# Blocks 2 and 3 of layer one by the seven-product scheme, with attention in another order and W2 jobs converted in another way

## The chip, the cores and the metric

One core of one Trainium2 chip. The metric is the time of one execution in device microseconds; a profile gives in addition the span from the first instruction to the last, the granted TensorE clock and the time of every instruction. TensorE multiplies, VectorE and ScalarE do elementwise work, GpSimd is nearly unused here, and every DMA of the stages below is issued from the SP queue.

## The reference

Chunked attention over 4 x 8 heads of 768 tokens (each chunk of 32 tokens sees 8 memory keys, 16 to the left, itself and 8 to the right), then two feed-forward layers over the 3072 tokens:

```python
scores = scale * np.matmul(q_c, k_full.transpose(0, 1, 3, 2))
a = np.exp(scores - np.max(scores, axis=-1, keepdims=True))
out[:, :, c_start:c_end] = np.matmul(a / (np.sum(a, axis=-1, keepdims=True) + 1e-09), v_full)
...
h = x @ w_in                                          # 3072 x 512 by 512 x 2048
g = np.maximum(h, 0.0) + np.log1p(np.exp(-np.abs(h))) # layer one, softplus
x = g @ w_out                                         # 3072 x 2048 by 2048 x 512
...
g = h - np.tanh(h)                                    # layer two, other weights
return g @ w_out
```

## The kernel before

**Numbers.** Weights, x and g are kept as two parts, a high part in the 32-bit format fp32r (`h`, `gh`) and a low part, the rest (`l`, `gl`). A product of two such operands is three matmuls, high by high, high by low, low by high (`mm3`, L368). Tokens lie in the free dimension, 512 to a block, so every big matmul is 128 x 128 by 128 x 512. `split_g` (L401) and `y_steps` (L677) make the parts of g: a cast on ScalarE gives `gh` (L405, L686), a subtraction on VectorE gives `gl` (L409, and L627 through `minus`). There are three buffers each of `gh` and `gl`.

**Layer one, plain.** For each of the 16 slices f of the hidden dimension, `ff_h` (L377) makes h (4 x 3 = 12 matmuls), ScalarE the softplus, `split_g` the parts, and `ff_y1` (L412) adds the slice's product with W1's output half into four PSUM tiles `ps_y` (12 matmuls). y runs LAG = 2 slices behind h. Blocks 0 to 3 run like this, block 0 inside a written opening.

**Seven products.** Where two blocks are taken together, y is a 2 x 2 block product by Strassen's scheme: seven products q, each over eight slices p instead of sixteen, on sums of the g quarters (`y_steps`, subtractions at L627) and on sums of weight quarters that jobs have stored in DRAM. `y_phase` takes 7 x 8 steps (q, p) of 6 matmuls. Before step s + 3's `gh`/`gl` are made, step s must have let its buffers go: `y_steps` is kept AHEAD = 3 steps ahead. After a product, `after_y` (L700) copies it (`kept`, ScalarE, L618) or adds it to the kept one (VectorE, L711) and stores it. The weight quarters come through a ring of 1 MB halves (`Ring`, L583), each loaded when the half before it in the same buffer is done (DMA of L601). Before, blocks 4 and 5 of layer one and all of layer two run by seven products; h of layer two does too, h of layer one does not. For blocks 4 and 5 all of h is made first (`steps`), into six rotating PSUM tiles, then y.

**Ticks.** The work that isn't the two layers' main stream is laid out by `tick` (L765), called once after every 12 big matmuls; the tables of numbers give the tick of everything:
- attention units 8 to 23 (128 tokens each): scores `s_mm` (L270) and the v product of the unit before (L343) in a unit's first tick, max and subtraction on VectorE (L295, L299), exp on ScalarE (L309) in the next, sum and scaling (L312 to L315) in the third, transposes `t_mm` (L320) and their copy `pT` (L332) in the fifth, x's parts (L358, L360) when the v product is there. A unit takes six ticks; softplus and exp need different tables on ScalarE (ACT_TABLE_LOAD). Units 20, 21 and 22 stand early in the order, and their x goes through DRAM.
- W1 jobs (`job_w1`, L488), which make the sums of W1's quarters; W2 jobs (`job_w`, L441), which load 1 MB of 64-bit floats of layer two's weights, rebuild 32-bit ones from their two words, split and store them, once as they are and once as sums (`split_to`, L428: cast L430, subtraction L434); x jobs (`job_x`, L500), which make the seven sums of layer two's x.

DVE, ACT, PE and SP run in the order in which the code issues. The jobs' results go through a pool of four buffers `o`; a buffer is free again when its store has landed. The W2 job before:

```python
nc.scalar.mul(c.bitcast(F32), hi.bitcast(F32), EXP_BIAS)                     # L450, ScalarE
nc.vector.tensor_scalar(out=c, in0=c, scalar1=3, ...)                        # L452
for of, k, op in ((hi, 0x80000000, and), (lo, 29, logical_shift_right)):
    nc.vector.scalar_tensor_tensor(out=c, in0=of, scalar=k, in1=c, ...)      # L454, twice
```

## Time and profile before

| | |
|---|---|
| median of 3 runs | 1059.66 us (1058.99 to 1059.68) |
| the profiled execution | 1059.62 us |
| its span | 1057.8 us |
| granted TensorE clock, mean | 0.998 |
| TensorE / VectorE / ScalarE busy | 1045.9 / 727.9 / 566.0 us |
| DMA | 303.19 MB, mean 287 GB/s |

The span is what the profile covers; the time of the execution is 1.8 us longer. Busy time of an engine is the union of its instructions. In lists of groups the columns are busy time, mean duration of one, and the idle time of the engine just before them with what ended it; matmuls overlap, so the mean of one matmul (389 ns) is longer than the distance of two.

### The profile page before, as it was taken

The numbers are of one execution on the slowest core, as the hardware profiler recorded it, in microseconds if no ns is written. First come the engines' busy times: TensorE is split into PE (matmuls) and PEld (weight loads), VectorE is DVE, ScalarE is ACT, GpSimd is POOL, SyncE is SP. The second block draws the span as 40 slices with busy tenths as digits, with TensorE's granted clock in tenths as the row PEclk, the third lists the DMA queues.
The fourth block names the chain that finished last, engine by engine and source line by source line (L and its number), as shares of the span: only waits on it lengthen the run. The fifth ranks groups of instructions, "written<-read, shape, count | busy, mean of one in ns | idle before, by whom it ended". The sixth has DMA issues, their size and how long they took to land.

```text
span 1057.8 us, 18468 instructions
## 1 busy us (share of the span) xinstructions
PE 1045.9 (99%) x7380; PEld 856.0 (81%) x7380; DVE 727.9 (69%) x1130; ACT 566.0 (54%) x901; POOL 4.4 (0%) x10
## 2 busy tenths in 40 slices
PE   7999999999999999999999999999999999999998
PEld 4788788888888888888888888888888888888886
DVE  5999355855755657487677688777487877446876
ACT  5996554655555455344555565545455554344553
POOL 1000000000000000000000000000000000000000
PEclk9999999999999999999999999999999999999999
DMA  9999955857776986999988999978899888746661
GB/s 309 409 368 347 350 190 180 285 195 227 265 250 234 308 313 199 356 337 342 327 339 295 351 369 348 342 286 324 285 356 346 287 324 290 246 164 211 244 206 60
DMA packets 101749, 303.19 MB, mean 287 GB/s; under 512 B 8096, under 2 KB 55200, under 8 KB 84000
## 3 DMA queue, kind: packets, MB, share of 16 engines
q1 hardware_dynamic: 101280, 300.97, 79.6%
q10 hardware_dynamic: 384, 1.05, 0.4%
q8 instruction: 58, 0.95, 0.4%
q14 instruction: 27, 0.22, 0.1%
HBM read 211.29 MB, written 90.70 MB: 285 GB/s over the span
## 4 chain that ended last, share of the span: by engine, by line
PE 95%; DMA 2%; ACT 1%; DVE 1%; issue 0%; ACTq 0%; DVEq 0%
PE ps_y L370 46%; PE ps_h L370 31%; PE ps_b L370 13%; PE ps_a L343 2%; PE ps_a L270 1%; DMA w<-in_qk 1%; PE ps_a L320 1%; DMA w<-in_w1i 1%; DMA y1d<-o 0%; PE ps_h L382 0%; PE ps_h L859 0%; ACT sm L304 0%; ACT x L304 0%; ACT x L358 0%; DVE st L295 0%; DVE c L495 0%
## 5 line engine op out<-in xcount | busy, mean ns | idle before, releaser
L370 PE MATMUL ps_h<-x,w 128*128 128x512 f32 x900 | 215.4, 390 | 0.0
L686 ACT CAST gh<-w 128x512 fp32r<-128x512 f32 x224 | 139.3, 623 | 140.0 <-DVE gl L627 120.0
L627 DVE TENSOR_TENSOR gl<-w,gh 128x512 fp32r<-128x512 f32 x236 | 162.8, 691 | 70.4 <-ACT gh L686 64.0
L370 PEld LDWEIGHTS ps_h<-x,w 128*128 128x128 f32 x900 | 168.6, 188 | 35.6 <-ACT t L393 0.3
L370 PE MATMUL ps_y<-gh,w 128*128 128x512 f32 x512 | 173.3, 399 | 0.1
L370 PEld LDWEIGHTS ps_y<-gh,w 128*128 128x128 f32 x512 | 96.1, 188 | 21.7 <-DVE o L423 0.5
L370 PE MATMUL ps_y<-gh,x 128*128 128x512 f32 x352 | 109.3, 389 | 0.0
L370 PE MATMUL ps_y<-gl,w 128*128 128x512 f32 x256 | 99.9, 390 | 0.0
L370 PE MATMUL ps_y<-w,x 128*128 128x512 f32 x402 | 94.5, 389 | 0.0
L370 PEld LDWEIGHTS ps_y<-w,x 128*128 128x128 f32 x402 | 75.5, 188 | 15.6
L409 DVE TENSOR_TENSOR gl<-t,gh 128x512 fp32r<-128x512 f32 x64 | 43.8, 687 | 53.0 <-ACT gh L405 52.7
L650 ACT ACTIVATE tanh<-sum 128x512 f32<-128x512 f32 x72 | 45.5, 632 | 59.9 <-DVE sum L623 59.8
L370 PEld LDWEIGHTS ps_y<-gh,x 128*128 128x128 f32 x352 | 66.1, 188 | 13.7
L393 ACT ACTIVATE t<-ps_h 128x512 f32<-128x512 f32 x64 | 38.2, 597 | 67.5 <-PE ps_h L370 66.8
L370 PE MATMUL ps_b<-gh,x 128*128 128x512 f32 x176 | 68.5, 389 | 0.0
L370 PE MATMUL ps_h<-gh,x 128*128 128x512 f32 x176 | 68.5, 389 | 0.0
L370 PE MATMUL ps_y<-gl,x 128*128 128x512 f32 x176 | 68.5, 389 | 0.0
L430 ACT CAST o<-c 128x1024 fp32r<-128x1024 f32 (+1 forms) x32 | 31.0, 969 | 69.8 <-DVE c L475 40.5
L627 DVE TENSOR_TENSOR w<-w 128x512 f32<-128x512 f32 x88 | 60.5, 688 | 7.1 <-ACT w L393 6.1
L370 PEld LDWEIGHTS ps_y<-gl,w 128*128 128x128 f32 x256 | 48.2, 188 | 9.2 <-DVE gl L409 0.3
L370 PE MATMUL ps_y<-x,w 128*128 128x512 f32 x240 | 55.2, 389 | 0.0
L370 PE MATMUL ps_b<-w,x 128*128 128x512 f32 x216 | 54.8, 389 | 0.0
(156 smaller groups left out, 1608.1 us busy)
## 6 DMA issues: line engine op xcount, KB each, us to landing
x<-wod SPq DMA_DIRECT2D x44, 1024.0 KB, 4.9
w<-x2d SPq DMA_DIRECT2D x21, 1024.0 KB, 7.0
x<-wid SPq DMA_DIRECT2D x21, 1024.0 KB, 6.6
wod<-o SPq DMA_DIRECT2D x32, 512.0 KB, 6.3
qk<-in_qk SPq DMA_DIRECT2D x21, 768.0 KB, 6.5
x2d<-o SPq DMA_DIRECT2D x30, 512.0 KB, 7.3
x<-wid SPq DMA_DIRECT2D x18, 768.0 KB, 6.8
ring<-wod SPq DMA_DIRECT2D x12, 1024.0 KB, 5.9
```

The costliest lines, as they stand in the source:

```text
L270: nc.tensor.matmul(out=ps[cc, j, KEYS * p : KEYS * (p + 1)], lhsT=a["q"][r, p, cc], rhs=a["k"][r, c, p, :], start=True, stop=True,)
L320: nc.tensor.transpose(ps[:, p * P : (p + 1) * P], a["sm"][:, p].rearrange("p j k -> p (j k)"), ident)
L343: nc.tensor.matmul(out=ps[h : h + 64, p % 2, 2 * P + t0 : 2 * P + t0 + CHUNK], lhsT=a["v"][r, c, p, :], rhs=a["pT"][r, p, CHUNK * c : CHUN ...
L370: nc.tensor.matmul(out=ps, lhsT=a, rhs=b, start=first and i == 0, stop=last and i == 2, skip_group_check=on,)
L393: nc.scalar.activation(out=out, in_=x, func=AF.Softplus)
L409: nc.vector.tensor_tensor(out=gl, in0=t, in1=gh.bitcast(F32), op=ALU.subtract)
L430: nc.scalar.copy(out=hi, in_=src)
L627: nc.vector.tensor_tensor(out=out, in0=x, in1=y, op=ALU.subtract)
L650: nc.scalar.activation(out=t, in_=h, func=AF.Tanh)
L686: nc.scalar.copy(out=gh, in_=src)
```

## The change

- **Blocks 2 and 3** leave the plain loop. All of their h comes first (32 times 12 matmuls, ticks 32 to 65, beside the last two y slices of block 1), the second block's slices in reversed order; y follows by seven products (`y_phase(0, ...)`, ticks 65 to 93). The ring of this phase is five of the W1 buffers; as they come free they are filled with the W1 input slices for blocks 4 and 5.
- **Attention** runs in natural order, with unit starts from a table: six or eight ticks a unit up to tick 32, four in ticks 32 to 60, then 5, 7, 10 and 9. In four-tick units the transposes stand in the fourth tick. Only unit 20 goes through DRAM.
- **W2 jobs** rebuild the floats by three operations on ScalarE and one on VectorE; inside the y phases of layer one (`Y_TICKS`) the three are a tick apart. **W1 jobs** all run in ticks 2 to 27 and use an `o` buffer for their sums. All jobs have other ticks. W1's input slices come from DRAM by table (`T1_LOADS`).
- Layer two and blocks 4 and 5 compute as before. In all there are 322 ticks for 326.

**The order on TensorE, layer one's h.** Before, in block 2 (ps_h and ps_y take turns; the numbers are buffers):

```order
L370 MATMUL ps_h_81<-x_1803,w_728 128x512 x12
L320 MATMUL ps_a<-ident,sm 128x128 x4
L370 MATMUL ps_y_686<-gh,w_635 128x512
L370 MATMUL ps_y_686<-gl,w_635 128x512
L370 MATMUL ps_y_686<-gh,w_635 128x512
```

Now, in block 2, with attention between:

```order
L377 MATMUL ps_y_688<-x_1809,w_2306 128x512 x12
L350 MATMUL ps_a<-pT,v 64x32 x32
L277 MATMUL ps_a<-qk 32x64 x32
L377 MATMUL ps_y_689<-x_1809,w_2306 128x512 x12
L377 MATMUL ps_h_81<-x_1809,w_2403 128x512 x12
L377 MATMUL ps_h_82<-x_1809,w_2403 128x512 x12
L327 MATMUL ps_a<-ident,sm 128x128 x4
L377 MATMUL ps_y_686<-x_1809,w_2575 128x512 x12
```

The y slices are gone from between the h slices, h uses all six tiles, and a unit's transposes and v product stand closer together.

**The order on VectorE around a W2 job.** Before, in the plain loop (`c` is the job's tile, `st` and `sm` the softmax):

```order
L409 TENSOR_TENSOR gl<-t,gh 128x512
L434 TENSOR_TENSOR o<-c_1862,o 128x768
L472 TENSOR_TENSOR c_1862<-c_1862 128x256
L473 TENSOR_TENSOR c_1862<-c_1862 128x256
L474 TENSOR_TENSOR c_1862<-c_1862 128x256
L475 TENSOR_TENSOR c_1862<-c_1862 128x256
L312 TENSOR_REDUCE st<-sm 128x8
```

Now, ticks 72 to 74, in the y of blocks 2 and 3:

```order
L646 TENSOR_TENSOR gl<-w_3922,gh 128x512
L730 TENSOR_TENSOR o<-ps_y_687,t 128x512
L441 TENSOR_TENSOR o<-c_4102,o 128x768
L485 TENSOR_TENSOR c_4102<-c_4102 128x256
L486 TENSOR_TENSOR c_4102<-c_4102 128x256
L487 TENSOR_TENSOR c_4102<-c_4102 128x256
L488 TENSOR_TENSOR c_4102<-c_4102 128x256
L646 TENSOR_TENSOR gl<-w_3922,gh 128x512
L646 TENSOR_TENSOR w_3923<-w_3050 128x512
L730 TENSOR_TENSOR o<-ps_y_689,t 128x512
L646 TENSOR_TENSOR gl<-w_3923,gh 128x512
L319 TENSOR_REDUCE st<-sm 128x8
```

The job's pieces, the evacuations of `ps_y` and a softmax stand between subtractions `gl` of neighbouring steps, six matmuls each.

**The order on ScalarE around a W2 job in a four-tick unit** (ticks 37 to 39; `w` tiles hold g, the exp of the unit stands just ahead):

```order
L458 ACTIVATE c_2895<-w_2726 128x1024
L461 ACTIVATE c_2895<-w_2726,low_bias 128x1024
L464 ACTIVATE w_2726<-w_2726 128x1024
L400 ACT_TABLE_LOAD
L400 ACTIVATE w_2886<-ps_h_82 128x512
L400 ACTIVATE w_2912<-ps_y_686 128x512
L437 CAST o<-c_2895 128x768
L400 ACTIVATE w_2936<-ps_y_687 128x512
L339 COPY pT<-ps_a 128x512
```

Before, a W2 job had one such operation (`L450 ACTIVATE`) two or more ticks from a `pT`; now three stand ahead of one.

The core of the diff:

```diff
-ATT_STEP = 6
-ATT_ORDER = (8, 9, 10, 11, 20, 12, 13, 14, 15, 21, 16, 17, 18, 19, 22, 23)
-VIA_DRAM = (20, 21, 22)
+ATT_AT = (0, 6, 12, 18, 26, 32, 36, 40, 44, 48, 52, 56, 60, 65, 72, 82, 91)
+ATT_FROM = 2 * UB
+VIA_DRAM = (20,)
...
+T1_SLOT = (0, 4, 3, 2, 1, 5, 6, 0)
+T1_RING = (1, 2, 3, 4, 0)
+W1_ORDER = (7, 0, 4, 3, 2, 1, 5, 6)
 JOBS = (
-    (1, 15, 24, 43, 53, 76, 85, 94),
-    (5, 14, 23, 33, 66, 75, 84, 92, 95, 99, 102, 106, 109, 113, 117, 152),
-    (42, 54, 159, 169, 214, 224),
+    (2, 8, 6, 14, 17, 22, 27, 26),
+    (8, 16, 28, 33, 49, 54, 59, 64, 94, 97, 100, 103, 109, 114, 133, 149),
+    (38, 112, 156, 169, 206, 222),
 )
...
+T1_LOADS = {9: 0, 13: 1, 17: 2, 21: 3, 25: 4, 29: 5, 33: 6, 38: 7, 54: 0}
+Y_TICKS = ((64, 94), (124, 154))
+PHASES = ((1, 1), (1, 2)) + tuple((2, b) for b in range(NT))
...
     def job_w(kind, p, second=False):
+        apart = any(a < now[0] + LEAD <= b for a, b in Y_TICKS)
...
-        c = pool.tile([P, 4 * HALF], U32, name=name, bufs=1)
-        nc.scalar.mul(c.bitcast(F32), hi.bitcast(F32), EXP_BIAS)
-        yield
-        nc.vector.tensor_scalar(out=c, in0=c, scalar1=3, scalar2=None, op0=ALU.logical_shift_left)
-        for of, k, op in ((hi, 0x80000000, ALU.bitwise_and), (lo, 29, ALU.logical_shift_right)):
-            nc.vector.scalar_tensor_tensor(
-                out=c, in0=of, scalar=k, in1=c, op0=op, op1=ALU.bitwise_or
-            )
+        x = pool.tile([P, 4 * HALF, 2], U16, name=name, bufs=1)
+        nc.scalar.mul(x[:, :, 1].bitcast(F16), hi.bitcast(F32), SIGN_ONLY)
+        if apart:
             yield
+        nc.scalar.activation(out=x[:, :, 0], in_=lo, func=AF.Identity, scale=LOW_SCALE, bias=low_bias)
+        if apart:
+            yield
+        nc.scalar.mul(hi.bitcast(F32), hi.bitcast(F32), EXP_BIAS)
+        yield
+        c = x.rearrange("p n two -> p (n two)").bitcast(U32)
+        nc.vector.scalar_tensor_tensor(
+            out=c, in0=hi, scalar=3, in1=c, op0=ALU.logical_shift_left, op1=ALU.bitwise_or
+        )
+        yield
...
-        for j in range(1, PLAIN):
...
+        steps = [(0, f) for f in range(NF)] + [(1, f) for f in reversed(range(NF))]
+        prepared = []
+        prep = y_steps(prepared)
+        ring = Ring((0,), ())
+        for n, (t, f) in enumerate(steps):
+            h_step(n, n == len(steps) - 1, t, f, x_tile(2 + t))
+            if pend:
+                run_y()
+                tick()
+            if t and f % 2 == 0 and f < 2 * T_RING:
+                s = T1_RING[T_RING - 1 - f // 2]
+                defer(lambda s=s: ring.add(wpool.tile([P, 2048], F32R, name=f"w{s}")))
...
+        y_phase(0, prep, prepared)
```

## Rows read from the trace of the kernel before

**Rows 1.** Page, busy time, share of the span and instructions of each engine.
```profile
PE 1045.9 (99%) x7380; PEld 856.0 (81%) x7380; DVE 727.9 (69%) x1130; ACT 566.0 (54%) x901; POOL 4.4 (0%) x10
```

**Rows 2.** Waits of TensorE: line, releaser, us in total, times, longest.
```profile
PE ps_a L258 <- DMA w<-in_qk: 1.7, 1, 1.7
...
PE ps_a L320 <- DVE sm L315: 1.1, 1, 1.1
```

**Rows 3.** Timeline of TensorE, 100 to 145 us: start, us, instruction, [idle before].
```profile
117.98 0.63 PE L320 MATMUL ps_a<-ident,sm 128*128 128x128 f32 x4 [1.11 <-DVE sm L315]
```

**Rows 4.** Windows: PE, PEld, DVE, ACT, POOL busy, granted clock, DMA share, GB/s.
```profile
597.00:673.00 76.00, 76.00 (x337) 62.96 (x336) 59.39 (x94) 43.98 (x76) 0.00 (x0) 1.00 0.96 351
```

**Rows 5.** Chain that ended last: start, us, what.
```profile
148.20 2.96 PE ps_y L370 x12
...
167.09 2.97 PE ps_y L370 x12
...
673.26 76.16 PE ps_y L370 x336
```

**Rows 6.** Timeline of VectorE, 160 to 180 us.
```profile
167.74 0.69 DVE L295 TENSOR_REDUCE st<-ps_a 128x8 f32<-128x512 f32 x1 [4.92 <-ACT x L358]
...
169.07 0.68 DVE L360 TENSOR_TENSOR x<-ps_a,x 128x512 fp32r<-128x512 f32 x1
169.67 0.68 DVE L409 TENSOR_TENSOR gl<-t,gh 128x512 fp32r<-128x512 f32 x1
170.27 0.95 DVE L434 TENSOR_TENSOR o<-c,o 128x768 fp32r<-128x768 f32 x1
171.14 0.42 DVE L472 TENSOR_TENSOR c<-c 128x256 f32<-128x256 f32 x1
...
172.73 0.68 DVE L312 TENSOR_REDUCE st<-sm 128x8 f32<-128x512 f32 x1
...
173.89 0.69 DVE L315 TENSOR_TENSOR sm<-sm,st 128x512 f32<-128x512 f32 x1
176.50 0.69 DVE L409 TENSOR_TENSOR gl<-t,gh 128x512 fp32r<-128x512 f32 x1 [1.92 <-ACT gh L405]
```

**Rows 7.** Groups of ScalarE by form: count, busy us, mean ns, idle before.
```profile
L686 ACT CAST gh<-w 128x512 fp32r<-128x512 f32 x224 | 139.3, 623 | 140.0 <-DVE gl L627 120.0
L393 ACT ACTIVATE t<-ps_h 128x512 f32<-128x512 f32 x64 | 38.2, 597 | 67.5 <-PE ps_h L370 66.8
L309 ACT ACT_TABLE_LOAD x19 | 24.4, 1283 | 0.3
L450 ACT ACTIVATE c<-w 128x1024 f32<-128x1024 f32 x12 | 13.6, 1131 | 5.1 <-DVE o L434 5.1
L332 ACT COPY pT<-ps_a 128x512 f32<-128x512 f32 x20 | 11.6, 582 | 1.3 <-PE ps_a L320 1.3
L430 ACT CAST o<-c 128x768 fp32r<-128x768 f32 x12 | 10.0, 832 | 26.6 <-DVE c L454 20.5 <-DMA y1d<-o 6.1
L169 ACT ACTIVATE c<-w,low_bias 128x1024 uint16<-128x1024 uint32 x4 | 5.8, 1459 | 0.0
L168 ACT ACTIVATE c<-w 128x1024 f16<-128x1024 f32 x4 | 5.6, 1389 | 0.0
```

**Rows 8.** Groups of VectorE by form.
```profile
L627 DVE TENSOR_TENSOR gl<-w,gh 128x512 fp32r<-128x512 f32 x236 | 162.8, 691 | 70.4 <-ACT gh L686 64.0
```

**Rows 9.** Timeline of ScalarE, 165 to 176 us.
```profile
169.19 0.63 ACT L309 ACTIVATE sm<-sm 128x512 f32<-128x512 f32 x1 [0.18 <-DVE sm L299]
...
175.84 0.62 ACT L405 CAST gh<-t 128x512 fp32r<-128x512 f32 x1
```

**Rows 10.** DMA issues: queue, count, KB each, median us to landing.
```profile
w<-in_w1i SPq DMA_DIRECT2D x16, 512.0 KB, 10.4
...
w<-in_w2i SPq DMA_DIRECT2D x8, 1024.0 KB, 7.4
wid<-o SPq DMA_DIRECT2D x16, 512.0 KB, 6.9
```

More of the change, by code (lines that the diff above doesn't have):

```diff
@@ L1 @@
+from bisect import bisect_right
 from contextlib import ExitStack
@@ L606, in get, with kept @@
         def get(self, u):
-            assert uses[self.used] == u
+            assert self.uses[self.used] == u
             return self.at[u].rearrange("p (i s n) -> p i s n", i=4, s=2)
         def done(self):
-            u = uses[self.used]
-            if last_use[u] == self.used:
+            u = self.uses[self.used]
+            if self.last_use[u] == self.used:
                 self.add(self.at.pop(u))
             self.used += 1
-    def kept(ps):
-        t = lpool.tile([P, N], F32, name="kept", bufs=4)
+    def kept(ps, d=0, q=0):
+        if lpool is not None:
+            t = lpool.tile([P, N], F32, name="kept", bufs=4)
+        elif q != 6:
+            t = tpool.tile([P, N], F32, name="t")
+        else:
+            if not d:
+                held["pair"] = tpool.tile([P, 2, N], F32, name="c2", bufs=1)
+            t = held["pair"][:, d]
         nc.scalar.copy(out=t, in_=ps)
@@ L703, in after_y @@
         if q in (1, 6, 5):
-            held[d, q] = kept(ps)
+            held[d, q] = kept(ps, d, q)
             return
@@ L723, in y_phase @@
         for i, q in enumerate(PRODUCTS):
-            ps = [banks[(2 * b + d) % 4][i % 2] for d in range(2)]
+            ps = [(banks[2 * (b - 1) + d & 3] if b else ps_y[2 * d : 2 * d + 2])[i % 2] for d in range(2)]
             for p in range(NP):
@@ L731, in y_phase @@
                 ring.done()
-                if p == NP // 2 and b + 1 < len(PHASES):
+                if not b and p % 4 == 3 and i * 2 + p // 4 >= 9:
+                    s = i * 2 + p // 4 - 9
+                    defer(t_load, s, s)
+                if p == NP // 2 and b and b + 1 < len(PHASES):
                     x2_load(PHASES[b + 1][1], q)
@@ L752, in attention_ffn_ffn @@
     T_W1, T_W2, T_X = JOBS
-    for t, p in zip(T_W1, (7, 0, 1, 2, 3, 4, 5, 6)):
+    for t, p in zip(T_W1, W1_ORDER):
         plan.setdefault(t, []).append(lambda p=p: job_w1(p))
@@ L784, in tick @@
             run(soft.pop(("x", before)))
+        if k in T1_LOADS:
+            t_load(T1_LOADS[k], T1_SLOT[T1_LOADS[k]])
         active.extend(job() for job in plan.get(k, ()))
@@ L792, in tick @@
             s_mm(u, ps_a)
-        if r == 4 and u is not None:
+        t = min(4, ATT_AT[i + 1] - ATT_AT[i] - 1) if u is not None else -1
+        if r == t:
             t_mm(u, ps_a[:, 0, :])
         next(chain, None)
-        if r == 4 and u is not None:
+        if r == t:
             t_out(u)
@@ L928, in act_g, with h_step @@
                 minus(g, g, g0)
-        for n, (t, f) in enumerate(steps):
-            ps = ps_h[(slot + n) % 2] if n < 4 else (*ps_y, *ps_h)[(n - 4) % 6]
+        def h_step(n, last, t, f, x):
+            ps = ps_h[n % 2] if n < 4 else (*ps_y, *ps_h)[(n - 4) % 6]
             weights["i", f] = w1t["i", f]
-            ff_h(f, ps, xs[t])
+            ff_h(f, ps, x)
             if f < NP and not t:
@@ L945, in attention_ffn_ffn @@
                 tick()
-            if n == 0:
-                xs[1] = x_tile(PLAIN + 1)
-                nc.sync.dma_start(
-                    out=xs[1].bitcast(F32).rearrange("p k s n -> p (k s) n")[:, :, : P * len(VIA_DRAM)],
-                    in_=x1d.rearrange("p k s n -> p (k s) n")[:, :, : P * len(VIA_DRAM)],
-                )
-            if now[0] > AT_END + 1 and lpool is None:
+            if t and f % 2 == 0 and f < 2 * T_RING:
+                s = T1_RING[T_RING - 1 - f // 2]
+                defer(lambda s=s: ring.add(wpool.tile([P, 2048], F32R, name=f"w{s}")))
+        late_x = x_tile(2 * NT - 1).bitcast(F32).rearrange("p k s n -> p (k s) n")
+        defer(
+            nc.sync.dma_start, late_x[:, :, : P * len(VIA_DRAM)],
+            x1d.rearrange("p k s n -> p (k s) n"), more=3,
+        )
+        y_phase(0, prep, prepared)
+        steps = []
+        for f in range(NF + T_LAG):
+            steps += [(0, f)] * (f < NF) + [(1, f - T_LAG)] * (f >= T_LAG)
+        prepared = []
+        prep = y_steps(prepared)
+        for n, (t, f) in enumerate(steps):
+            x = x_tile(2 * (NT - 1) + t)
+            h_step(n, n == len(steps) - 1, t, f, x)
+            if now[0] > ATT_AT[-1] + 1 and lpool is None:
                 attention.close()
```

102 lines of the change are left out of this document (45 added, 57 removed).

## The prediction

> **What bounds the kernel now.** I read the busy shares first: TensorE is busy 99% of the span [rows 1]. Busy is not yet bound, so the waits on TensorE came next: eight groups of one wait each, the longest for the first loads, one of 1.1 us for a softmax result [rows 2]. That one is the last, at 118 us [rows 3]; behind 125 us the view has no row. The window of a later stage, the first h of layer two, says the same: TensorE 76.00 of 76.00 us at a granted clock of 1.00, the 2.4 GHz level, with VectorE at 59.39 us and ScalarE at 43.98 [rows 4]. The chain prices the work: 336 matmuls of 512 columns in 76.16 us, 0.2267 us each [rows 5]. So time is the number of matmuls, as long as VectorE and ScalarE stay ahead. The profiled execution took 1059.62 us, of which the span is 1057.8; it lies 0.04 under the median of the runs, 1059.66, and I work from it.
>
> **What the change takes away.** For two 512-token blocks plain y is 2 x 16 x 4 x 3 = 384 matmuls; the scheme needs 7 x 8 x 2 x 3 = 336. The built program agrees: big matmuls into ps_h fall from 1536 to 1296, into ps_y they rise from 2184 to 2376. 48 x 0.2267 = **10.88 us** less, all on the path. h keeps its 2 x 192 matmuls. The sixteen attention units keep their matmuls too: six ticks with one unit took 167.09 - 148.20 = 18.89 us [rows 5], 72 x 0.2267 = 16.32 of it big matmuls, so 2.57 us a unit (2.15 in its first tick, 0.42 for the transposes) wherever it stands. The opening stands word for word as before on every queue, so its waits stay.
>
> **What it adds on the path.** The new y of blocks 2 and 3 runs in ticks 65 to 93, with attention units 21 to 23 and two W2 jobs inside. By its average it fits: VectorE gets 56 gl subtractions, 24 sums and 8 evacuation adds or copies, at most 88 x 0.60 = 52.8 us; the attention units 3 x 3.7 and the job pieces some 8.5 (2 x 2.46, below, and three operations twice as wide at twice 0.60), together 72.4 us in 76.16 + 3 x 2.57 = 83.9 us. The price of 0.60 is from the queue when it has no wait: starts at 169.07, 169.67 and 170.27, though each operation is 0.68 long [rows 6].
>
> But the work comes in bunches, and a step here is short: 6 x 0.2267 = 1.36 us. There are three gh/gl pairs, so the pair of step n+3 can be cast only when step n has finished. Cast 0.62 [rows 7], subtraction 0.69 [rows 8], two hand-overs of about 0.04 (the cast of 175.84 ends at 176.46 [rows 9], its subtraction starts at 176.50 [rows 6]): 1.4 us. It is needed by the second matmul of step n+3, 2 x 1.36 + 0.23 = 2.95 us after step n. The margin is 1.55 us; whatever stands ahead of a subtraction beyond this and the 0.76 us that a step leaves free, TensorE waits for. Pieces by the starts [rows 6]: low half of three parts 171.14 - 170.27 = 0.87, four sums 172.73 - 171.14 = 1.59, together 2.46; first half of a softmax with its x (max, subtract, xl) 169.67 - 167.74 = 1.93; second half 173.89 - 172.73 + 0.60 = 1.76.
>
> *Ticks 66 and 67.* The 2.46 stand ahead of step 5's subtraction: 2.46 - 0.76 - 1.55 = 0.15 over. The next pair gains 0.16. Then 1.76 + 0.60 - 1.36 = 1.00, less 0.16, over at step 7. About **1.0 us**.
> *Ticks 72 to 75.* The first half of unit 22 has its 2.15 us of attention matmuls as cover. Behind step 18's subtraction stand an evacuation add (0.60) and 2.46: 0.60 + 2.46 + 0.60 - 1.36 - 1.55 = 0.75 over. A sum and the second add before step 20: 3 x 0.60 - 1.36 = 0.44. The second half before step 21: 1.00. About **2.2 us**.
>
> *Buffers of the o pool.* Four are rotated, and the low half in tick 68 takes the one whose store SP issues in tick 66, behind a ring half, two attention loads and the x1d store; the buffer is wanted about 9.5 us later. Such a store of 512 KB landed in 6.9 us in the median, the loads of the crowded opening in 10.4 [rows 10]. Bounds 0 (6.9) and 4 us (twice 6.9, 13.8); nearest to the crowded rows I take **1.0 us**. The same job in the second y (ticks 140 to 144), without attention, passes the margin by at most 0.1.
>
> **What lies beside.** A W2 job gives ScalarE three operations (1.39 + 1.46 + 1.13 = 3.98 us) for one of 1.13 [rows 7], 45.6 us more over 16 jobs, and VectorE one operation for three. In the four-tick units (ticks 37, 53, 58) the three stand ahead of a pT copy that TensorE wants. Counted from the unit's first tick: attention matmuls 2.15, max and subtract 1.33, exp 0.63 and hand-overs give 4.2; then 3.98, a table load 1.28, three softplus 1.8, cast 0.83, pT 0.58: 12.7 [rows 6, 7, 9]. The v matmuls stand at 4.87 + 2.72 + 2.72 + 3.14 = 13.45. Spare 0.75 us: taken at nothing. If the cover goes (a W2 load 2 us late) it is 1.25 us at each of three places, 3.8 in all; they load 13 us ahead and land in 7.4 [rows 10].
> The eight W1 jobs crowd into ticks 2 to 27 and put up to 7 us of VectorE work in one tick of 2.72; block 1's gl is wanted four ticks, 10.9 us, behind its h, so nothing. In the h-only ticks six PSUM tiles rotate, five ticks of room for a softplus: nothing. On the SP queue and the DMA engines 14 ring halves and 9 W1 loads come, 4 others go, about 20 MB on 303; each ring half has four halves, 4 x 5.44 us, to land: nothing.
>
> **Sum:** 1059.62 - 10.88 + 1.0 + 2.2 + 1.0 + 0.1 = **1053.0 us**.
>
> **Rivals.**
> *VectorE's operations do not overlap.* If an operation starts only when the one ahead has ended, each of the some 22 free successions in the two bunches costs 0.09 more (0.69 for 0.60), 2.0 us: 1055.0. Against it: the starts in [rows 6]. For it: successions where one reads the other's result, which took 0.72 and more. Chance 0.12.
> The Trainium skill, VectorE: DVE Perf Modes, section The DRAIN you can't avoid, says that the next operation does not start until the pipeline has emptied, and that leaving out semaphores does not skip this; by it the sum is this rival's 1055.0. The trace does not bear it out for independent operations, and the page itself exempts an instruction that is not held.
> *No wait at all.* The stage of [rows 4] has no wait with VectorE at 78%, and here ScalarE and VectorE may run ahead further than I count: 1059.62 - 10.88 = 1048.7, up to 1050.5. Against it: the stage of [rows 4] has no attention. Chance 0.15.
> *The o buffers decide, and it ends slower.* In tick 74 the cast of the high half, on ScalarE ahead of two gh casts, takes the buffer whose store goes out after step 15's ring half, and wants it about 7 us later. With a landing time L the two places cost (L - 9.5) + (L - 7). Against 10.88 - 3.2 = 7.7 us left, that decides from L = 12.1 us; at twice the median, 13.8, it is 11.1 us: 1063.0. For it: SP is one queue, and stores stand behind loads that wait for TensorE. Against: the crowded opening saw 10.4. Chance 0.05 for slower, 0.08 for a landing between, which ends within 0.2%.
> That the change does not do what it says is ruled out by the counted matmuls.
>
> **Numbers.** My forecast, waits of 2 to 6 us in all, 1050.5 to 1055, has 0.60, and 1053.0 is its middle. A measurement tells about 0.2%, 2.1 us, from no change. Faster: 0.60 + 0.15 + 0.12 = 0.87; within 0.08; slower 0.05. Range 1049.0 to 1057.0: it takes in most of the no-wait case and the non-overlapping VectorE with two more microseconds of late stores.
>
> **What would show it.** 7332 matmuls for 7380 and big ones still 0.2267 us apart. New waits of TensorE for gl, 3 to 4 us in all, in two clusters early in the new y stage, none in the second y or layer two. Layer two's first h started at 597 us [rows 4]; the new stage starts 88 ticks of 2.72 us and 9.9 us of attention ahead of it, and all of it comes 10.9 sooner, so at about 337: the clusters lie near 342 and 363 us. VectorE without a pause there, starts 0.60 apart. A VectorE wait for a store in the first cluster, about 1 us. I am wrong if TensorE waits for pT in the h-only ticks, for a ring half, or for layer two's sums, or if the waits are over 8 us.

## The result, and the profile after

The changed kernel takes **1076.51 us** (median of 4 runs, 1074.25 to 1076.60), the kernel before 1059.67 beside it: ratio 1.015, 95% interval 1.0137 to 1.0162. I had predicted 1053.0 with a range to 1057. It is slower by 16.8 us where I forecast faster by 6.7. The profiled execution took 1076.6 us, its span is 1074.8.

The page of the changed kernel, busy time, answers to [rows 1]:

```profile
PE 1046.0 (97%) x7329; PEld 851.7 (79%) x7332; DVE 733.8 (68%) x1157; ACT 613.1 (57%) x956; POOL 4.4 (0%) x10
```

There are 48 matmuls fewer (7332 by the weight loads; three records of matmuls are missing), and yet TensorE is as long busy as before and idle besides. Its waits from 120 us on, where the kernel before has none behind [rows 3] (line, releaser, us in total, times, longest):

```profile
PE ps_y L377 <- ACT gh L705: 5.2, 3, 2.5
PE ps_a L327 <- DVE sm L322: 4.4, 2, 2.7
PE ps_y L377 <- DVE gl L646: 2.5, 5, 0.9
PE ps_a L350 <- ACT pT L339: 2.5, 1, 2.5
PE ps_a L277 <- issue: 1.0, 1, 1.0
PE ps_b L377 <- DVE gl L646: 0.4, 1, 0.4
```

That is 16.0 us. The timeline of TensorE has the large ones, in three stretches: 223, 258 to 264, and 368 to 395 us, the last inside the new y of blocks 2 and 3 (start, us, instruction, idle before):

```profile
223.59 0.63 PE L327 MATMUL ps_a<-ident,sm 128*128 128x128 f32 x4 [2.67 <-DVE sm L322]
...
257.97 0.63 PE L327 MATMUL ps_a<-ident,sm 128*128 128x128 f32 x4 [1.78 <-DVE sm L322]
263.89 0.32 PE L350 MATMUL ps_a<-pT,v 64*64 64x32 f32 x8 [2.53 <-ACT pT L339]
359.25 0.50 PE L377 MATMUL ps_y<-gl,w 128*128 128x512 f32 x1 [0.61 <-DVE gl L646]
362.82 0.50 PE L377 MATMUL ps_y<-gl,w 128*128 128x512 f32 x1 [0.56 <-DVE gl L646]
368.61 0.80 PE L377 MATMUL ps_y<-gh,w 128*128 128x512 f32 x1 [2.53 <-ACT gh L705]
388.85 0.50 PE L377 MATMUL ps_y<-gl,w 128*128 128x512 f32 x1 [0.92 <-DVE gl L646]
394.42 0.51 PE L377 MATMUL ps_y<-gh,w 128*128 128x512 f32 x1 [2.34 <-ACT gh L705]
```

The other part is the clock. Windows of 4 us behind those waits (TensorE busy, granted clock, DMA share, GB/s):

```profile
224.00:228.00 4.00, 4.00 (x13) 0.59 0.80 230
...
264.00:268.00 4.00, 4.00 (x133) 0.71 0.95 297
268.00:272.00 4.00, 4.00 (x17) 0.86 1.02 372
368.00:372.00 4.00, 3.39 (x7) 0.51 1.05 401
372.00:376.00 4.00, 4.00 (x13) 0.63 0.64 213
392.00:396.00 4.00, 1.44 (x5) 0.93 1.07 319
396.00:400.00 4.00, 4.00 (x15) 0.65 0.96 356
```

1.00 is the 2.4 GHz level, and a window near 0.5 stands wholly at 1.2. One minus the clock, times the busy time, summed over all windows behind 120 us, gives 8.1 us. So 16.0 + 8.1 = 24.1 of the 27.9 us by which the profiled execution exceeds 1059.62 - 10.88 = 1048.7. Most of the remainder lies at the same waits, which cost more than their listed idle time (worked out at the end of the section on the prediction).

What TensorE waits for in the large ones was itself held up, each time by a store that had not landed. VectorE and ScalarE; four of the rows wait for a store, those at 250.85 and 366.76 us for a VectorE that has waited:

```profile
218.60 1.36 DVE L508 TENSOR_TENSOR o<-w 128x256 f32<-128x256 f32 x3 [2.84 <-DMA wid<-o]
...
247.56 0.69 DVE L430 COPY o<-ps_y 128x512 f32<-128x512 f32 x1 [6.64 <-DMA y1d<-o]
...
250.85 1.05 ACT L437 CAST o<-c 128x1024 fp32r<-128x1024 f32 x1 [8.24 <-DVE c L488]
...
365.45 1.23 DVE L441 TENSOR_TENSOR o<-c,o 128x1024 fp32r<-128x1024 f32 x1 [1.48 <-DMA x1d<-o]
...
366.76 1.34 ACT L458 ACTIVATE c<-w 128x1024 f16<-128x1024 f32 x1 [5.42 <-DVE o L441]
...
392.80 1.04 ACT L437 CAST o<-c 128x1024 fp32r<-128x1024 f32 x1 [5.80 <-DMA wid<-o]
```

Each of the four writes a tile of the four-buffer pool `o`, whose buffer is free only when the store of its last content has landed. At 218.60 it is a W1 job's sums, with unit 12's softmax queued behind. At 247.56 it is the last of the four copies of `out1`, which takes block 1's finished y out of PSUM; behind it come the low half, the sums (which the cast at 250.85 waits for), then unit 13's x and unit 14's softmax. At 365.45 it is a low half; ScalarE's first operation of the next W2 job waits for it, as both use the one buffer `c2`, and the gh cast stands behind that. At 392.80 it is a high half, with gh casts behind. The chain shows the stores of the last two places (start, us, what):

```profile
355.00 10.43 DMA x1d<-o
...
385.85 6.88 DMA wid<-o
```

The second was late before it began. The tile was written at 379.37 us, but the SP queue, which issues in order, stood ahead of its store with two ring halves that wait for TensorE to finish with their buffers (the view of waits has SP waiting 13.2 us for `ps_y` there, in two waits):

```profile
376.12 7.85 SPq L613 DMA_DIRECT2D w<-wod  x2
...
379.37 0.83 ACT L437 CAST o<-c 128x768 fp32r<-128x768 f32 x1
...
385.39 0.95 SPq L446 DMA_DIRECT2D wid<-o  x2
```

The tile is complete at 380.20 and its store goes out 5.2 us later. With the same 7 us to land, a store issued at once would have been in by about 387 us, and the cast at 392.80 has its input only at 388.19, when the sums end; that is an estimate, no run moved the store alone.

### The profile page after: what moved, and what is told of

Read it like the earlier page. It is cut to its first block, busy times and chain, and to the rows that moved or that the text cites. A ratio compares the mean times of both kernels' runs of the same rounds, so it can differ in the third digit from the quotient of the medians.

```text
span 1074.8 us, 18518 instructions
## 1 busy us (share of the span) xinstructions
PE 1046.0 (97%) x7329; PEld 851.7 (79%) x7332; DVE 733.8 (68%) x1157; ACT 613.1 (57%) x956; POOL 4.4 (0%) x10
## 4 chain that ended last, share of the span: by engine, by line
PE 62%; DVE 2%; DMA 2%; ACT 1%; issue 1%; ACTq 0%; SPq 0%
PE ps_y L377 36%; PE ps_h L377 14%; PE ps_b L377 11%; DVE gl L646 1%; DMA x1d<-o 1%; ACT gh L705 1%; DMA wid<-o 1%; DVE w L646 0%; PE ps_a L350 0%; DVE c L467 0%; DVE o L441 0%; PE ps_a L277 0%; PE ps_a L327 0%; ACT kept L637 0%; DVE o L367 0%
## 5 line engine op out<-in xcount | busy, mean ns | idle before, releaser
L705 ACT CAST gh<-w 128x512 fp32r<-128x512 f32 x280 | 173.0, 622 | 167.4 <-DVE gl L646 121.6
L646 DVE TENSOR_TENSOR gl<-w,gh 128x512 fp32r<-128x512 f32 x292 | 201.0, 690 | 84.7 <-ACT gh L705 78.0
L377 PE MATMUL ps_y<-gh,w 128*128 128x512 f32 x480 | 161.9, 406 | 4.9 <-ACT gh L705 4.9
L377 PE MATMUL ps_h<-x,w 128*128 128x512 f32 x660 | 157.9, 391 | 0.0
L377 PEld LDWEIGHTS ps_h<-x,w 128*128 128x128 f32 x660 | 123.1, 188 | 26.4 <-DVE w L200 0.3
L377 PE MATMUL ps_y<-x,w 128*128 128x512 f32 x480 | 114.4, 395 | 0.0
L377 PEld LDWEIGHTS ps_y<-x,w 128*128 128x128 f32 x480 | 90.6, 190 | 19.1
L646 DVE TENSOR_TENSOR w<-w 128x512 f32<-128x512 f32 x104 | 71.5, 688 | 31.5 <-ACT w L400 30.4
L642 DVE TENSOR_TENSOR sum<-ps_y,kept 128x512 f32<-128x512 f32 x36 | 24.8, 690 | 44.0 <-PE ps_y L377 35.1
L646 DVE TENSOR_TENSOR w<-w,w 128x512 f32<-128x512 f32 x80 | 54.8, 685 | 0.0
```

The lines of the kernel that those rows point to most:

```text
L377: nc.tensor.matmul(out=ps, lhsT=a, rhs=b, start=first and i == 0, stop=last and i == 2, skip_group_check=on,)
L642: nc.vector.tensor_tensor(out=h, in0=ps, in1=t, op=ALU.add)
L646: nc.vector.tensor_tensor(out=out, in0=x, in1=y, op=ALU.subtract)
L705: nc.scalar.copy(out=gh, in_=src)
```

## Experiments

The theory: a buffer of `o` is wanted before its store has landed, urgent work is queued behind the engine that waits, TensorE runs dry, and its clock falls. The rivals: VectorE and ScalarE have too much work in the denser attention, or in the three-operation conversion. The code lines in the diffs are those of the changed kernel. The ratios are against the kernel before, run beside each on the same chip (medians 1060.1 to 1060.6, for 1059.67 beside the changed kernel), so differences of a microsecond from 1076.51 are not read. "Less" is less than 1076.51.

**One buffer at a time.** Four edits, each against the changed kernel.

```diff
 # c1_out1_pairs, in out1
-            o = opool.tile([P, N], F32, name="o")
+            if e % 2 == 0:
+                pair = opool.tile([P, 2, N], F32, name="o")
+            o = pair[:, e % 2]
 # c2, c3 and c4: the 4 KB that they need
-            sm = apool.tile([P, NPAIR, 2, KEYS], F32, name="sm")
+            sm = apool.tile([P, NPAIR, 2, KEYS], F32, name="sm", bufs=1)
-            pT = apool.tile([P, NPAIR, P], F32, name="pT", bufs=1)
+            pT = apool.tile([P, NPAIR, P], F32, name="sm", bufs=1)
 # c2_x1d_apart, in x_out
-            x = opool.tile([P, KT, 2, P], F32R, name="o")
+            x = apool.tile([P, KT, 2, P], F32R, name="xd", bufs=1)
 # c3_w1_sums_apart, in job_w1 and JOBS
-        c = opool.tile([P, 4, HALF], F32, name="o")
+        c = apool.tile([P, 4, HALF], F32, name="c1", bufs=1)
-    (2, 8, 6, 14, 17, 22, 27, 26),
+    (2, 8, 6, 14, 17, 22, 27, 24),
 # c4_five_o; four again (pool o2) once attention has ended
-    opool = ctx.enter_context(tc.tile_pool(name="o", bufs=4))
+    opool = attention.enter_context(tc.tile_pool(name="o", bufs=5))
```

> The four copies of block 1's y use two o buffers (two copies side by side in one) where they used four; nothing else is changed. Theory (the four o buffers are held until their stores land, TensorE then runs out of work, and its clock falls behind the wait): the three waits of TensorE between 247 and 264 us (0.99, 1.78 and 2.53 us) go, and with them the stretch of lowered clock behind the last (windows 264 to 272 at 0.71 and 0.86, worked out as 1.7 us): 7.0 us less, about 1069.5 us; the waits at 223, 368 and 394 stay. Rival (the three ScalarE operations of the W2 job stand ahead of pT, whatever the buffers do): the 2.53 us wait for pT and its clock stay, at most 2.8 us go, 1073.7 or more. Rival (VectorE and ScalarE have too much work in a tick): no change, 1076.5.

Measured: 1072.65 us (1.0108, 1.0093 to 1.0123), 3.9 less. The wait for a softmax at 258 us is gone, the one for pT is 1.17 us and the clock behind it stays at 1.00; those at 226, 366 and 390 us stay. So more than half of what the three ScalarE operations ahead of pT cost came from the buffers, which had made them late. Of the 7.0 us expected, 4.9 are gained at this place (240 to 280 us, matmul against matmul). The rest of the difference lies elsewhere: the opening, which the edit leaves alone, took 2.4 us more in the profiled execution (a wait for a softmax result at 117.81 us stands at 120.17 here; the windows of 24 to 32 us have a clock of 0.77 and 0.50 for 1.00), and behind the waits at 226 and 366 us less was lost to the clock. In c8, with the same edit, the opening took no longer.

> Unit 20's x tile, the one that is stored to x1d, has a buffer of its own (4 KB won by giving a unit's softmax and pT one buffer, whose uses follow each other anyway); the four o buffers no longer hold the x1d store. Theory: VectorE's wait of 10.4 us for the x1d store in tick 68 goes, and with it TensorE's wait of 2.53 us at 368 us and the lowered clock behind it (windows 368 to 376 at 0.51 and 0.63, 3.4 us): 5.9 less, about 1070.6; the wait at 394 us (2.34 and 1.4) may go too, as the rotation there moves by one buffer: down to 1066.9. Rival (gh is late because ScalarE and VectorE have too much to do in ticks 66 to 74): no change, 1076.5, the gh waits stay.

Measured: 1076.03 (1.0138, 1.0113 to 1.0162): no gain in the time. In the trace the gh wait behind tick 68 is 0.98 us for 2.53 and the clock there stays at 1.00, as the theory says; but the buffer that softmax and pT now share, which I had called free, made three new waits for pT (0.41, 0.70, 1.44 us) and one of 0.88 ahead of the transposes, 3.4 us in all, and the gh wait of tick 74 stays (2.22).

> The W1 jobs' sums have a buffer of their own (the same 4 KB), as they had before the change, and no longer one of the four o buffers; the job at tick 26 starts at 24, since two jobs in ticks 26 and 27 would want the one buffer. Theory: VectorE's wait of 2.84 us for a store at 218.6 us goes, and with it TensorE's wait of 2.67 us at 223 us and the lowered clock behind it (window 224 to 228 at 0.59, 1.6 us): 4.3 less, about 1072.2. Rival (the W1 jobs crowd VectorE whatever the buffers do): the softmax of unit 12 stays late, 1076.5.

Measured: 1074.46 (1.0137, 1.0118 to 1.0156), not clear of the changed kernel's interval; the reading is the trace's. The wait at 223 us and its clock are gone, as expected (window 220 to 232 at 1.00); the shared buffer takes 3.4 us back, and the wait at out1's place is 2.75 us for 1.78.

> Five o buffers for four while attention runs (the 4 KB as above), all else as in the changed kernel. Theory: each of the four places waits for a store that lands a few us too late; a fifth buffer puts off each by one use, so the waits at 223, 247 to 264, 368 and 394 us go or fall below 1 us, and with them the lowered clock: 20.9 us less, about 1055.6, between 1050 and 1062. Rival (the bunching of VectorE and ScalarE, or the three-operation conversion): no change, 1074 to 1077. Rival (the DMA queue itself is too slow, so the fifth buffer is late too): about half, 1066.

Measured: 1068.92 (1.0078, 1.0063 to 1.0093), 7.6 less and no lowered clock behind 120 us, but not 1055.6. (Here too the opening took more, 1.7 us in the profiled execution; from 120 us on 9.1 less.) The fifth buffer doesn't reach at out1, where six are wanted in three ticks: a low half still waits 6.4 us for a y1d store, and TensorE 2.60 and 2.21 us at 256 and 262.

**Is it the load?** Three edits, and a sum of two.

```diff
 # c5_jobs_moved, JOBS
-    (8, 16, 28, 33, 49, 54, 59, 64, 94, 97, 100, 103, 109, 114, 133, 149),
+    (8, 16, 28, 33, 49, 54, 94, 97, 100, 103, 109, 114, 124, 133, 141, 149),
 # c6_old_conversion: job_w's ScalarE and DVE operations as before the change
 # c7_attention_six
-ATT_AT = (0, 6, 12, 18, 26, 32, 36, 40, 44, 48, 52, 56, 60, 65, 72, 82, 91)
-VIA_DRAM = (20,)
+ATT_AT = tuple(range(0, 97, 6))
+VIA_DRAM = ()
 # c8_out1_and_moved: c1 and c5
```

> The two W2 jobs that the change starts at ticks 59 and 64 (their o buffers are wanted in ticks 65 to 75, inside the new y stage) start at 124 and 141 instead, inside the second y, where no attention runs; the order of the sixteen jobs stays. Theory (o buffers, with urgent casts queued behind the engine that waits): the waits of TensorE for gh at 368 and 394 us (2.53 and 2.34 us) go with the lowered clock behind them (3.4 and 1.4 us), and of the gl waits (2.5 us in all) what the jobs' pieces add, about half: 9.7 to 11 us less, 1065.5 to 1067. Rival (attention and the gh/gl pairs alone are too much for ScalarE and VectorE there): the gh waits stay, at most 1 us less, 1075.5. Rival (the jobs cost as much wherever a y stage takes them): the waits come back between 420 and 540 us, 1073 or more.

Measured: 1077.25 (1.0154, 1.0134 to 1.0174); the last rival was right about the time. The waits at 368 and 394 are gone and come back in the second y, without attention. The timelines of ScalarE and, under it, TensorE:

```profile
554.38 1.04 ACT L437 CAST o<-c 128x1024 fp32r<-128x1024 f32 x1 [6.49 <-DMA wod<-o]
...
607.83 1.04 ACT L437 CAST o<-c 128x1024 fp32r<-128x1024 f32 x1 [5.88 <-DMA y1d<-o]
```

```profile
556.00 0.51 PE L377 MATMUL ps_b<-gh,ring 128*128 128x512 f32 x1 [3.00 <-ACT gh L705]
...
609.44 0.80 PE L377 MATMUL ps_b<-gh,x 128*128 128x512 f32 x1 [3.05 <-ACT gh L705]
```

It is the same cast, and again an `o` buffer: at ticks 124 and 141 the jobs' buffers fall among the evacuations of y, as at 64. The job at 133, between two pairs of evacuations, cost 0.4 us in the changed kernel.

> The W2 jobs' conversion as before the change (one ScalarE operation and three of VectorE, for three of ScalarE and one of VectorE), in the same ticks; all else as changed. Theory (o buffers): the waits for sm at 223 us, for gh at 368 and 394 us stay; the wait for pT at 264 us gets shorter by what two of the three ScalarE operations take that stand ahead of pT (2.53 to about 0), with the clock behind it: 1072 to 1076.5. Rival (the three-operation conversion overloads ScalarE): the gh waits go as well, 1066 or less. Rival (VectorE is the short one): slower than the changed kernel, 1077 or more, with more gl waits.

Measured: 1075.07 (1.0134, 1.0119 to 1.0149), as the theory said. The wait for pT moved from 264 to 280 us (2.26), the gh wait at 370 stays (2.22), the second became a gl wait of 1.83.

> Every attention unit gets six ticks, as before the change, instead of four to nine; unit 20 is then late enough to write its x straight into the block's x tile, so the x1d store and its load fall away. The W2 and W1 jobs and the o buffers stay as changed. Theory (o buffers): the wait at 368 us gets shorter since no x1d store holds a buffer, the others may move by a tick or two but stay in kind: out1's copies and the W1 sums still hold up the casts behind them, though a softmax may not be queued behind them any more, as the units start at other ticks (30, 36, 42): 1066 to 1075. Rival (density of attention is the cause): the waits go nearly all, 1050 to 1056.

Measured: 1076.89 (1.0155, 1.0138 to 1.0173). Neither: it is not the density, but nor was it any milder. A pT copy now stands behind a W1 job's high cast that waits 6.2 us, and TensorE waits 5.30 us for it at 228 us; in the y stage gh is 3.16 and 5.10 late.

> Both: out1's copies in two o buffers (1072.65 us by itself) and the two W2 jobs moved to ticks 124 and 141. Theory: the two act in places 100 us apart, so their gains add up: 1076.5 - 3.9 - 9.7 to 11 = 1062 to 1063; what is left above the count of matmuls (1048.7) is the wait at 226 us (2.78 and its clock), small pT waits and the gl waits without jobs. Rival (gh waits from attention): 1072.

Measured: 1072.05 (1.011, 1.0095 to 1.0125): c1's gain alone, as c5 by itself gave none.

**Two ticks.** One number of JOBS: `59, 64,` becomes `59, 66,`.

> One number: the W2 job of tick 64 starts at 66. Its high cast of the last four parts then takes an o buffer whose store was issued three ticks before, not one (the two evacuations of ticks 72 and 73 now come ahead of the job's buffers). Theory (o buffers): the gh wait at 394 us (2.34 us) goes or falls below 0.5, with the lowered clock behind it (1.4 us): 3.7 less, 1072.8; all other waits stay. Rival (a W2 job in a y stage is too much for ScalarE): the gh wait stays and moves by two ticks, 1076.5.

Measured: **1067.67** (1.0061, 1.0048 to 1.0075), 8.8 less. Both gh waits went, not one: the waits of TensorE for gh are 0.6 us in all for 5.2. The first had needed two things, the late store and the next job's operation waiting on ScalarE for `c2`. Two ticks later that operation isn't due yet, and in this trace the store isn't late either: it landed in 8.07 us for 10.43, and VectorE found its buffer free. What fits is that the moved job's raw tile (`w<-in_w2i`, 1 MB), issued 5 us ahead of the x1d store before (350.06 and 355.00 us), now goes out behind it (355.24 and 353.88); no run moved that load alone.

**Schedules by a rule.** The same four buffers, sums and conversion, out1 in pairs, and other ticks: no `o` buffer is to be wanted within three ticks of its store's issue where something urgent is queued behind. One thing goes with the ticks: unit 20 now ends late enough to write its x in place (`VIA_DRAM = ()`), so the x1d store and its load back fall away. The sixth, against the changed kernel:

```diff
-ATT_AT = (0, 6, 12, 18, 26, 32, 36, 40, 44, 48, 52, 56, 60, 65, 72, 82, 91)
-VIA_DRAM = (20,)
+ATT_AT = (0, 6, 12, 18, 24, 30, 35, 40, 44, 48, 52, 56, 60, 67, 74, 82, 91)
+VIA_DRAM = ()
-    (2, 8, 6, 14, 17, 22, 27, 26),
-    (8, 16, 28, 33, 49, 54, 59, 64, 94, 97, 100, 103, 109, 114, 133, 149),
-    (38, 112, 156, 169, 206, 222),
+    (2, 8, 6, 14, 19, 22, 11, 27),
+    (8, 16, 25, 32, 37, 53, 59, 66, 94, 97, 100, 103, 109, 114, 133, 149),
+    (43, 112, 156, 169, 206, 222),
-T1_LOADS = {9: 0, 13: 1, 17: 2, 21: 3, 25: 4, 29: 5, 33: 6, 38: 7, 54: 0}
+T1_LOADS = {9: 0, 13: 1, 17: 2, 21: 3, 25: 4, 33: 5, 35: 6, 38: 7, 54: 0}
```

> The changed kernel with the same four o buffers, the same sums and the same three-operation conversion, but the numbers of the schedule chosen by one rule: wherever attention or gh/gl pairs are queued behind, an o buffer is wanted again no sooner than three ticks after its store was issued (8.2 us). out1's copies take two buffers; W1 jobs of ticks 26 and 27 start at 27 and 31; W2 jobs of 28, 33, 49, 54, 59, 64 at 31, 36, 53, 58, 66 and 126; the first x job at 43 for 38; units start at 24, 30, 35 for 26, 32, 36, at 61 and 67 for 60 and 65, by which unit 20 needs no x1d. Theory (o buffers): the waits at 223, 247 to 264, 368 and 394 us go (0 to 3 us left), and so does the lowered clock; the gl clusters stay at 1 to 2.5 us: 1048.7 plus 2 to 6, 1051 to 1055, faster than the kernel before. Rival (attention and jobs load ScalarE and VectorE too heavily in any order): 1065 or more.

Measured: 1066.68 (1.0051, 1.0037 to 1.0065). All four places are clean, but TensorE waits 2.32 us for gh at 342 us and about 2.5 at 554 to 562, each with a lowered clock.

> The new schedule with the two places mended where it still showed TensorE waiting: at 342 us a W2 job's three ScalarE operations (tick 62) stood ahead of a softplus and of unit 20's softmax, so the jobs of ticks 58 and 126 start at 59 and 165 (in layer two's h, where nothing urgent is queued behind), unit 20 at 60 again, and one x job at 170 for 169. Theory (o buffers and the order on the engines that wait for them): the gh wait of 2.32 us at 342 us with its clock (3.4 us) and those at 554 to 562 us (2.5 us with a clock of 1.7) go: 1066.7 - 9.9, about 1056 to 1057, faster than the kernel before by 3 to 4 us. Rival (ScalarE and VectorE are overloaded in the stretch with attention and y): new waits of the same size elsewhere, 1064 or more.

Measured: 1069.1 (1.0089, 1.0071 to 1.0107), the profiled run 1066.2. The waits at 554 to 562 us are gone, of those at 339 to 342 us 1.70 are left, without a lowered clock, and the job put into layer two's h costs 5.9 us of waits there and a lowered clock.

> The second schedule with one number put back: the W2 job of tick 66 starts at 64, as in the changed kernel, so its last high cast takes an o buffer whose store was issued one tick before. Theory (o buffers): a gh wait of 2 to 3 us near 385 us returns with a lowered clock behind it: 4 to 9 us above the second schedule (the same number alone gave 8.8 us on the changed kernel). Rival (the two ticks don't matter by themselves): within 1.5 us of the second schedule.

Measured: 1069.99 (1.0095, 1.0078 to 1.0112), 0.9 above. This one went against me in the time. In the trace the mechanism is back: the high cast waits for its store, and TensorE waits 0.80 us for gh behind it and 1.63 for gl, ahead of which the late softmax pieces now stand: 2.43 in two pieces. ScalarE:

```profile
375.18 1.05 ACT L439 CAST o<-c 128x1024 fp32r<-128x1024 f32 x1 [4.22 <-DMA wid<-o]
```

But no single wait is of 2 us, and the clock doesn't fall there. Beside x1d out of the pool and units at other ticks the same two ticks were worth little; the price of one number isn't its own.

> The second schedule moved the sixteenth W2 job into layer two's h, and there it brought waits of its own (644 to 680 us: 1.79, 1.20, 0.76 and 2.13, and a lowered clock worth 1.6). Here that job stands in the h stage of blocks 4 and 5 (five jobs with the second pair of tiles at ticks 94, 99, 104, 109, 114 for four), where only softplus is queued behind, and the x job is back at 169. Theory: the first y stage stays as in the second schedule, the second y and layer two are as in the changed kernel, so 1066.2 - 1.79 - 1.20 - 0.76 - 2.13 - 1.6 = 1058.7, and by the landmark of the second y stage (a gl wait at 567.4 us, at 586.7 in the changed kernel, 483.8 ahead of the end of TensorE's work) 1057.2: 1056 to 1060, the kernel before within 0.3%. Rival (the wait moves on again, since the stores of 16 jobs need the four buffers somewhere): 1062 or more.

> The third schedule with the first x job and the W2 job behind it one tick later (44 and 54 for 43 and 53), so that the x job's casts start with a unit. Theory: the wait for sm of 0.67 us at 292 us goes or moves, nothing else: within 1.5 us of the third schedule.

Measured: 1077.61 (1.0157, 1.0141 to 1.0173) and 1076.49 (1.0147, 1.0131 to 1.0163). They are alike, as the second text said, but the first text's rival was right: one job more between the two y stages (the fifth with the second pair of tiles) is one too many for the buffers. In the third schedule's view of waits, ScalarE and TensorE from 440 to 560 us:

```profile
ACT o L439 <- DMA wod<-o: 14.4, 2, 9.3
```

```profile
PE ps_y L377 <- ACT w L400: 7.9, 4, 2.9
PE ps_b L377 <- ACT gh L707: 2.8, 1, 2.8
```

There softplus is what stands behind the casts; I had taken it for not urgent.

> The second schedule's first half (its stage up to the second y showed waits of 3.9 us and no lowered clock), with the sixteenth W2 job at tick 25, where the o buffers were not wanted for five ticks, and one W1 job at tick 11 for 31 to make room; from tick 94 on every number is as in the changed kernel, which showed there one wait of 0.42 us. Theory (o buffers are the whole loss): no wait is left that the second schedule's first half and the changed kernel's second half did not have, so the time is 1066.2 - 7.5 (the second schedule's waits in layer two with their clock) = 1058.7, by the landmark 1057.2: 1055 to 1060, at or just below the kernel before. Rival (it moves on again): a wait of 2 us or more between 190 and 270 us, 1062 or more.

Measured: 1065.23 (1.0043, 1.0029 to 1.0057), the rival: a raw tile came 4.32 us late for a W2 job (`w<-in_w2i`), whose operations stand ahead of a unit's x and softmax, and TensorE waited 3.64 us at 270 us.

> The fifth schedule with three numbers mended at its two remaining places: W2 jobs at 32 and 37 for 31 and 36, so that their three ScalarE operations stand behind a unit's exp and not ahead of its x cast (where a raw tile landed 4.3 us late and the softmax of unit 16 with it, TensorE waiting 3.64 us at 270 us), and the W1 job of tick 17 at 19, so that its cast does not wait 6.3 us for a store ahead of unit 11's x. Theory (o buffers and what is queued behind them are the whole loss): those waits (3.64 and 1.00 us) and the lowered clock behind them (1.3 us) go: 1065.2 - 5.9 = 1059.3, between 1057 and 1062. Rival (it moves on again): 1064 or more.

Measured: **1059.89** (12 runs; 0.9998, 0.9989 to 1.0008), as expected: level with the kernel before, 16.6 us below the changed one, with the same matmuls, jobs and conversion. Its page and its waits from 120 us on:

```profile
PE 1038.5 (98%) x7332; PEld 846.3 (80%) x7332; DVE 733.2 (69%) x1157; ACT 613.6 (58%) x956; POOL 4.4 (0%) x10
```

```profile
PE ps_y L377 <- DVE gl L648: 3.1, 6, 1.1
PE ps_a L327 <- DVE sm L322: 1.8, 2, 1.1
PE ps_y L377 <- ACT gh L707: 1.3, 3, 0.6
PE ps_a L277 <- issue: 0.5, 1, 0.5
PE ps_b L377 <- DVE gl L648: 0.4, 1, 0.4
PE ps_a L350 <- ACT pT L339: 0.3, 1, 0.3
```

VectorE and ScalarE are as busy as in the changed kernel (733.2 and 733.8, 613.6 and 613.1): the amount of work was not the cause. One window from 120 us to the last matmuls, of the changed kernel and of the sixth schedule, shows the whole difference (TensorE, its weight loads, VectorE, ScalarE, POOL, clock, DMA, GB/s):

```profile
120.00:1069.00 949.00, 932.57 (x6051) 765.05 (x6050) 637.56 (x1024) 523.05 (x792) 0.00 (x0) 0.99 0.81 293
```

```profile
120.00:1052.00 932.00, 924.52 (x6051) 759.73 (x6049) 636.93 (x1024) 523.49 (x792) 0.00 (x0) 1.00 0.82 297
```

The same 6051 matmuls. TensorE is idle 949.00 - 932.57 = 16.43 us in the one and 7.48 in the other, 8.95 less; and its busy time is 8.05 us shorter at a clock of 1.00, which is the 8.1 worked out from the windows above. Together that is the 17.0 us by which the window is shorter.

## Why the prediction was wrong, and where it was right

*The step that failed.* The count of matmuls held; the waits did not. The sum has 4.3 us of them, and the trace has 16.0 and 8.1 of lowered clock. Two terms were put at nothing and were the larger part: the operations ahead of pT, behind out1's copies (5.3 us of waits and 1.7 of clock), and the W1 jobs (2.7 and 1.6). Tick 68, put at 1.0, cost 2.5 and 3.1; tick 74, left to a rival with 0.05, cost 2.3 and 1.5. In each the sum asked whether an engine had time enough for its work, or priced the wait of that engine alone, and not what is queued behind it while a store holds its buffer.

*The count and its price: right.* 7332 matmuls; a stretch of layer two's h answers to [rows 4] with the same 337 in 76.00 us:

```profile
607.00:683.00 76.00, 76.00 (x337) 62.94 (x336) 53.49 (x86) 44.69 (x75) 0.00 (x0) 1.00 0.94 350
```

A four-tick unit without a wait takes 13.44 us from s to s (279.99 to 293.43), and 4 x 2.72 + 2.57 = 13.45 was assumed.

*Ticks 66 and 67, 1.0 us: right.* 0.61 + 0.56 = 1.17, at 359 and 363 us, behind the very pieces named (the four sums, then the softmax's second half). I had 342; 12 of the 17 us are the earlier waits with their clock, the other 5 I have not worked out.

*Ticks 72 to 75, 2.2 us: right in kind.* In the sixth schedule, where no store disturbs, the gl and gh waits of that bunch (380 to 388 us) are 0.55 + 0.56 + 0.26 + 0.23 = 1.6. It is not quite the same bunch: the job starts two ticks later there, and the unit as well. In the changed kernel 0.92 of it is seen before the 2.34 for gh covers the rest.

*The o pool in tick 68, "1.0 us", bounds 0 and 4: VectorE's wait was right, its price to TensorE wrong.* The buffer was wanted 9.0 us after the store's issue (365.45 - 1.48 - 355.00), where I had 9.5, and the store took 10.43 us, as in the crowded rows that I went by; it was that of x1d itself, not one behind it. VectorE's wait was 1.48. But another engine stood behind VectorE: ScalarE's next job operation wanted `c2`, the gh cast stood behind that, and TensorE paid 2.53 plus 3.1 of clock. With the x1d tile out of the pool (run c2) 0.98 is left, about 2.53 - 1.48: that part is the order on ScalarE, the rest the store.

*Tick 74: the forecast left it out, and the rival mis-timed it.* The cast "wants it about 7 us later" than the store goes out. ScalarE was free for it at 392.80 - 5.80 = 387.00 and its input there at 388.19, 1.2 and 2.3 us after the issue at 385.85: one tick lay between them. At that distance even a landing of 6.9 us costs 4.5; the condition L over 12.1 us was wrong, and so was the chance of 0.05. What the rival gave for itself, that stores stand behind loads that wait for TensorE on the one SP queue, is what the rows at 376 to 385 us show.

*"The W1 jobs ... so nothing": wrong.* I looked at gl alone, which has 10.9 us to spare. A softmax was queued behind the sums too, and the sums had moved into `o`: 2.67 us and a lowered clock. c3 takes it away.

*The three operations ahead of pT "at nothing": wrong by its cover.* I had named a late W2 load as what would take the cover away. It was out1: its four copies in `o`, unchanged by the diff, now fell among the buffers of the W2 job of tick 28 and ahead of a unit. I had not looked at them at all. c1 takes away the softmax wait and more than half of the one for pT; with one ScalarE operation for three (c6) both kinds of wait are still there, 2.32 us at 259 and 2.26 at 280, so the conversion isn't the cause.

*The clock: missing.* No term or rival had the lowered clock behind a wait. By the windows above it made the four places dearer by 1.6, 1.7, 3.1 and 1.5 us.

*The rivals.* That VectorE's operations don't overlap is out: in the new bunch they start 0.60 apart again (352.33, 352.93 and 354.25, 354.85 us, each 0.68 long). The Trainium skill, VectorE: DVE Perf Modes, section The DRAIN you can't avoid, has the next operation start only when the pipeline is empty, but earlier where it is not held. Starts of 0.60 for 0.68 of duration, of operations that don't read each other, agree with that exemption and not with the rule by itself. That no wait remains is out as well. The third, that the buffers decide, named the right resource and the right sign, in two of four places.

*What else was said.* No wait for a ring half, none in the h-only ticks for a softplus, and 0.42 us in the second y for the 0.1 I had: right in kind. In layer two, where I had no wait, stand 0.37 and 0.22 us at 693. Two marks of being wrong were met: "waits over 8 us" by twice, and TensorE waiting for pT in the h-only ticks, at 264 us.

Even the sixth schedule stays 10.5 us above 1048.7 (profiled 1059.25). 7.4 are the waits shown; the other 3.1 lie at the same waits. The view counts idle time from the end of the last matmul, 0.39 us after its start, while matmuls that don't wait start 0.23 apart, and the one behind a wait is followed 0.33 later. At 383.86 us:

```profile
382.69 0.61 PE L377 MATMUL ps_y<-gh,w 128*128 128x512 f32 x2
383.86 0.50 PE L377 MATMUL ps_y<-gl,w 128*128 128x512 f32 x1 [0.56 <-DVE gl L648]
384.20 0.63 PE L377 MATMUL ps_y<-gh,w 128*128 128x512 f32 x2
```

From 382.69 to 384.20 are 1.51 us for three distances, which take 0.68 without a wait: 0.83 lost where 0.56 is listed. Ten waits between big matmuls lose 2.6 us in this way and three ahead of attention matmuls 0.5; all other big matmuls stand as close as in the kernel before. So the 48 matmuls are real, and what is left of waits in the denser attention and in this y takes them back; whether a schedule exists that keeps part of them was not settled: none I ran was faster than the kernel before.

## What to carry to other kernels

For each tile of a rotated pool that is stored, write down when its store is issued and when the buffer is wanted again, over the whole pool, the unchanged users included; where that is under the landing time, list what is queued behind the waiting instruction on its engine, and on the other engine through any single buffer that both use. The issue is not the write: a store can stand for microseconds on its queue behind loads that wait for something else. The wait is paid where that work has the least slack, and it may be paid twice, in the clock. A gain in the count of matmuls is worth having only if the schedule is made again around it: the same change was 1.5% slower, and level with the kernel before once ticks were moved, copies put side by side in pairs, and with that one store to DRAM and its load had become needless.
